# Attention within clusters, then a gated MLP: another searched order of one scheduled kernel, with other engines for splits, casts and code copies

## The chip, the cores and the metric

The kernel runs on one core of one Trainium2 chip. The metric is the device time of one execution in microseconds (us); less is better. TensorE multiplies matrices (PE in the profile, its weight loads PEld), VectorE is DVE, ScalarE is ACT, GpSimd is POOL, and SyncE (SP) issues most of the transfers.

## The reference

There are 4 batches of 8 heads, 768 positions and 64 channels per head, and 16 cluster centres per head. Each query and each key is assigned to the centre with the largest cosine; a query sees only the keys of its own cluster. The attention's result, 3072 rows of 512, goes through an MLP without biases.

```python
q_assign = np.argmax(np.einsum('bhsd,hcd->bhsc', q_n, c_n), axis=-1)
k_assign = np.argmax(np.einsum('bhsd,hcd->bhsc', k_n, c_n), axis=-1)
mask = q_assign[:, :, :, None] == k_assign[:, :, None, :]
scores = np.where(mask, scale * np.matmul(q, k.transpose(0, 1, 3, 2)), -1e9)
attn = softmax(scores)
x = (attn @ v).transpose(0, 2, 1, 3).reshape(B * S, H * D)      # 3072 x 512
h = x @ w_in                                                    # 512 -> 2048
out = (h * (1.0 / (1.0 + np.exp(-h)))) @ w_out                  # 2048 -> 512
```

## The kernel before

**Splits and turns.** Heads are worked on in pairs (p from 0 to 3 in each batch). `load_k`, `load_q` and `load_v` bring a pair's rows in; `load_v`'s second step casts V to 16 bits (`vt`, L431 on ScalarE, L433 on GpSimd or VectorE). `part` makes a pair ready: `hi` writes the scaled 16-bit value (L550 ScalarE, L552 VectorE, L554 GpSimd) and `lo` the remainder (L558, VectorE) into `hl`. Then `hl` is turned, channels on the partitions, into `ab`. For batch 0 TensorE does this by transposes, and another engine casts the result out of PSUM: in blocks of 8 (L584, cast by L593 or L595), or the older way by way of `lt` (L617, cast by L632 or L634), in which the cluster codes are turned by TensorE too (L617 once more, cast with a gain by L628 or L630). For batches 1 to 3, a DMA turns it (L573).

**Codes.** `logits` (L667, L671; L676 for later batches) multiplies by the centres; VectorE finds the largest (L718, or L694 and L714) and marks it (L743, or L726 on GpSimd, L753, L755). The marks are turned 32 by 32 on VectorE (`flip`, L771), and four copies per part (`put`, L786 ScalarE, L788 and L790 GpSimd, L792 and L794 VectorE) place them on partitions 64 to 79 of `ab`. So one matmul over 80 rows gives score and mask together.

**Attention.** For each head `scores` (L861) fills a PSUM bank with 512 scores, ScalarE takes the exponential (L868) into `P`, `pv` (L889) multiplies by V with a column of twos for the sum, VectorE divides (L902, L907), and the pair is turned into `xt` by a DMA (L926) or by TensorE (L937, cast by L942 or L944). Batch 0 is done in two rounds over the queries, blocks 0 and 1 first (24 exponentials), then 2 to 5 (48), so that the MLP can begin early.

**MLP.** `up` (L967) makes 16 blocks of 128 hidden channels, `tanh` (L973, ScalarE) and `gate` (L978, VectorE) the activation into `gq`, `down` (L1002) the result, which `leave` takes out of PSUM (L1015 ScalarE, L1017 VectorE) and SyncE stores (L1020). There are nine units of rows: three of 256 in batch 0, then two of 384 in each batch.

**What sets the order.** The kernel adds about 2,200 steps to a planner (`Plan`), each with an engine, an estimated duration, the steps it follows, the buffers it uses, and a key. `Plan.order` plays them through: the step that can start first goes next, and of equal ones that with the lower key. The instructions are then issued in that order, so each engine's queue is fixed at build time. Keys come from due times: `AT` (start of each round of attention), `ML` (start and end of each MLP unit) and `LEADS` (how far ahead of its use a part is made). `REST`, `RLOAD` and `SOON` say at which head of the attention a later part or load is let go. Where the planner sees TensorE idle before `UNREAD`, it puts in matmuls on zeros that nobody reads (L369); `MORE` lengthens such a fill. `FLIP` is time that it adds to a transposing DMA.

**Weights.** `w_in` comes in 4 pieces and `w_out` in 8, issued by GpSimd (L1036, L1040). Each waits for an event by reading one column of a tile into `pace` (L1034): `PW` gives for each piece the number of its event, 0 to 4 the `hi` steps of batch 0's keys, from 5 on every second exponential in the order in which the steps were added.

**Engine choices.** `VC` for the casts of batch 0's V by pair; `TK` for the casts of the turned blocks (entries 0 and 1 for the heads of pair 0, 2 to 4 for pairs 1 to 3); `TQ` for the codes, a word of four letters for four copies (P GpSimd, D VectorE, A ScalarE), or an engine's name for codes that TensorE turns; `TF` an extra engine for the first turn of a head done the older way; `TR` and `TS` the same as `TK` and `TQ` for the later queries of batch 0; `HI` and `HR` for `hi`; `PUTB` for later batches' codes; `XT` for the cast after L937; `EVAC` for `leave`, by unit.

```python
blocks = turn != "DMA" and turn[1] not in ("ACT", "DVE")
first_turns = [(c, his + los, turn[0]) for c in chunks]
if len(turn) > 2 and turn[2]:
    cut = runs[1][4]
    first_turns = [(chunks[0][:cut], [his[0], los[0]], turn[0]), (chunks[0][cut:], [his[1], los[1]], turn[2])]
```

Of the kernel before, what the change touches and what calls it, by code (L numbers as in the profile page):

```python
# [34 lines left out]
class Plan:  # L35
# [18 lines left out]
    def step(self, eng, w, fn, after=(), use=(), key=0.0, load=None, hold=0.0, pace=None, flip=False, lag=None, slack=0.0, port=None):  # L54
        s = Step()
        s.eng, s.w, s.fn, s.key, s.load, s.hold, s.flip = eng, w, fn, key, load, hold, flip
        s.lag = self.LAG.get(eng, 0) if lag is None else lag
        s.slack = slack
        s.port = eng == "POOL" if port is None else port
        s.use = list(use)  # L60
        s.n = len(self.steps)
        flat = []

        def gather(a):
            if isinstance(a, (list, tuple)):
                for x in a:
                    gather(x)
            elif a is not None:
                flat.append(a)

        gather(list(after))
        gather(pace)
        s.after = list({id(x): x for x in flat}.values())
        s.start = s.end = None
        for b in s.use:
            b.left += 1
        self.steps.append(s)
        return s
# [130 lines left out]
def kernel(  # L209
# [80 lines left out]
    def buf(name):  # L290
        return Buf(pools[name])
# [15 lines left out]

    SMALL = 30
    ISSUE = 470
    PW = [9, 6, 17, 12, 20, 21, 12, 6, 13, 25, 37, 25]  # L310
    UNREAD = 60000.0
    COLD = 8500.0
    MORE = 250.0
    LATE = 1500
    FLIP = 1200
    DONE = 0
    WSL = 1000
    AT = [-428.5, 146.6, 377.7, 476.2, 674.4, 872.8]
    ML = [144.4, 478.9, 304.3, 486.1, 673.0, 923.5, 414.3, 31.2, 1085.3, 1156.6]
    PUTB = ["POOL", "DVE", "POOL", "POOL"]  # L320
    VC = ["ACT", "POOL", "POOL", "DVE"]
    VB = "POOL"
    TK = ["DVE", "ACT", "ACT", "DVE", "ACT"]
    TQ = ["PPPD", "PPPA", "DVE", "PPPA", "PPPD"]
    TF = ["ACT", ""]
    TR = ["ACT", "DVE", "DVE", "DVE"]
    TS = ["PDPD", "PPPD", "PPPA", "PDPD"]
    RT = ["PE", "PE", "PE", "PE"]
    HI = ["POOL", "ACT", "POOL", "POOL"]
    HR = ["DVE", "POOL", "DVE", "POOL"]  # L330
    LEADS = [1401.7, 519.0, 568.3]
    REST = [1, 1, 10, 7]
    RLOAD = [0, 0, 0, 0]
    SOON = [6, 6, 5, 4]
    XT = ["DVE", "DVE", "DVE", "ACT"]
    XL = ["DMA", "DMA", "DMA"]
    EVAC = ["ACT", "DVE", "DVE", "DVE", "DVE", "DVE", "DVE", "DVE", "DVE", "ACT"]
    SPARE = 0
    FINE = 2

# [31 lines left out]

    plan.filler = (pools["M"], lambda t: 180.0 if t < COLD else 112.0, unread, UNREAD, MORE)

# [22 lines left out]
    def load_q(b, p, key, j0=0, j1=NJ, eng="SP", hs=(0, 1), pace=None):  # L397
        if (b, p) not in nqs:
            nqs[b, p] = buf("nq")
        x = nqs[b, p]  # L400

        def f():
            e = nc.sync if eng == "SP" else nc.scalar
            h0, h1 = 2 * p + hs[0], 2 * p + hs[-1] + 1
            e.dma_start(T["nq"][x.i][:, hs[0] : hs[-1] + 1, j0 * D : j1 * D], rows(q, b, h0, h1, j0, j1))

        s = step(eng, ISSUE, f, use=[x], key=key, load=105 * (j1 - j0) * len(hs), pace=pace, slack=LATE if b else 550 if eng == "ACT" else 0)
        for h in hs:
            for j in range(j0, j1):
                ld_q[b, p, h, j] = s  # L410
        return s
# [3 lines left out]
    def load_v(b, p, key, pace=None):  # L415
        eng = VC[p] if b == 0 else VB
        x = buf("nv")

        def f():
            nc.sync.dma_start(T["nv"][x.i], rows(v, b, 2 * p, 2 * p + 2, 0, NJ))  # L420

        s = step("SP", ISSUE, f, use=[x], key=key, load=1250, pace=pace, slack=LATE if b else 0)
        for h in range(2):
            y = buf("vt")
            vts[b, 2 * p + h] = y

            def g(h=h, y=y):
                dst = T["vt"][y.i][:, 0 : NJ * VW].rearrange("p (j c) -> p j c", c=VW)[:, :, 0:D]
                src = T["nv"][x.i][:, h, :].rearrange("p (j d) -> p j d", d=D)
                if eng == "ACT":  # L430
                    nc.scalar.copy(dst, src)  # L431
                else:
                    (nc.gpsimd if eng == "POOL" else nc.vector).tensor_copy(dst, src)  # L433

            w = {"POOL": pool_w(384), "ACT": act_w(384), "DVE": dve_w(384, 0.55)}[eng]

            cast_v[b, 2 * p + h] = step(eng, w, g, port=eng == "DVE", after=[s, s_ones], use=[x, y], key=key + 20)
# [57 lines left out]
    def part(b, p, segs, a0, due, lead=20.0, hi_eng="POOL", turn="DMA", twin=False, sub="POOL", code_eng=None, pace=None, wait=None):  # L495
# [73 lines left out]
        if turn == "DMA":  # L569
# [4 lines left out]

            turned = [step("SP", 120 * n, turn_dma, after=[his, los], use=[hl, A], key=key + 2 * span, load=195 * n, flip=True, slack=FLIP)]
        elif blocks:
# [245 lines left out]
    def attention(b, h, j0, j1, key, per, turn):  # L822
# [100 lines left out]
        if turn == "DMA":  # L923
# [6 lines left out]

            x = step("SP", 1240, turn_x, after=done, use=[xn, X], key=key + per - 3, load=195 * nq, flip=True, slack=FLIP)
        else:
# [96 lines left out]
    def weight(kind, n, event):  # L1029

        x, use, name, col = event

        def f():
            nc.gpsimd.tensor_copy(pace, T[name][use.i][:, col : col + 1])  # L1034
            if kind == "in":
                nc.gpsimd.dma_start(  # L1036
                    win_s[:, :, ts(n, 512)], moe_w_in.rearrange("(r p) f -> p r f", p=128)[:, :, ts(n, 512)]
                )
            else:
                nc.gpsimd.dma_start(  # L1040
                    wout_s[:, 2 * n : 2 * n + 2, :],
                    moe_w_out[256 * n : 256 * n + 256, :].rearrange("(c p) d -> p c d", p=128),
                )

        return step("POOL", 1210, f, after=[x], use=[use], key=-1, load=2390 if kind == "in" else 1190, slack=WSL)


    want = {(n, h): AT[n] + (AT[n + 1] - AT[n]) * h / H for n in range(NU + B - 1) for h in range(H)}

# [14 lines left out]
    for h in range(2):  # L1064
        part(
            0, 0, [("k", h, 0, NJ), ("q", h, 0, NA)], (NJ + NA) * h, want[0, h], lead=LEADS[0], hi_eng=HI[0],
            turn=(TK[h], TQ[h], TF[h]), wait=s_split if h else None, **engines,
        )
    for p in range(1, NP):
        part(  # L1070
            0, p, [("k", 0, 0, NJ), ("k", 1, 0, NJ), ("q", 0, 0, NA), ("q", 1, 0, NA)], 0, want[0, 2 * p], lead=LEADS[0],
            hi_eng=HI[p], turn=(TK[1 + p], TQ[1 + p]), wait=s_cent, **engines,
        )
# [3 lines left out]
    def at(place, f):  # L1077
        todo.setdefault(place, []).append(f)

    for p in range(NP):  # L1080
        at(RLOAD[p], lambda s, p=p: load_q(0, p, want[1, 2 * p] - 30, NA, NJ, pace=s))
        at(
            REST[p],
            lambda s, p=p: part(
                0, p, [("q", 0, NA, NJ), ("q", 1, NA, NJ)], 2 * (NJ + NA), want[1, 2 * p], lead=LEADS[1], pace=s,
                hi_eng=HR[p], **(engines | dict(turn=(TR[p], TS[p])) if RT[p] == "PE" else dict(code_eng=PUTB)),
            ),
        )
    for b in range(1, B):
        for p in range(NP):  # L1090
# [3 lines left out]
            for f, early in ((load_k, 32), (load_q, 31), (load_v, 30)):  # L1094
                at(place - (SOON[0] if soon else SOON[1]), lambda s, b=b, p=p, f=f, due=due - early: f(b, p, due, pace=s))
            for i in range(2):
                at(
                    place + i - (SOON[2] if soon else SOON[3]),
                    lambda s, b=b, p=p, i=i: part(
                        b, p, [("k", i, 0, NJ), ("q", i, 0, NJ)], 12 * i, want[b + NU - 1, 2 * p + i], lead=LEADS[2], pace=s, code_eng=PUTB  # L1100
                    ),
                )
    for place in range(H * (B + NU - 1)):
        n, h = divmod(place, H)
        per = (AT[n + 1] - AT[n]) / H
        if n < NU:
            j0, j1 = ROUNDS[n]
            attention(0, h, j0, j1, want[n, h], per, XT[p] if (p := h // 2) == NP - 1 or n + 1 < NU else "DMA")
        else:
# [4 lines left out]
    for n in range(4):  # L1114
        w_in_done.append(weight("in", n, events[PW[n]]))
    for n in range(8):
        w_out_done.append(weight("out", n, events[PW[4 + n]]))
    units = [(0, *r) for r in UNITS] + [(b, 3 * c, 3 * c + 3) for b in range(1, B) for c in range(2)]
    for n, (b, j0, j1) in enumerate(units):
        mlp(b, j0, j1, ML[n], ML[n + 1], lambda t, n=n: EVAC[n], n == len(units) - 1)  # L1120

# [31 lines left out]
```

## Time and profile before

| | us |
|---|---|
| median of 3 runs | 304.93 (304.78 to 305.57) |
| the profiled execution's own time | 306.86 |
| its span, first to last instruction | 304.9 |
| TensorE busy in the span | 295.9 |
| VectorE, ScalarE, GpSimd busy | 216.5, 216.4, 124.5 |
| granted TensorE clock | 1.00 throughout |

The profile is of one execution. "Busy" is the time in which an engine has at least one instruction under way; matmuls overlap, so a row's mean duration is longer than the distance from one start to the next. A row of the timeline gives start, length, engine, line, operation, output<-inputs, shapes, the number of instructions merged, and in brackets the idle time before it with what ended it. A row of the groups gives busy time and mean length, then the idle time before the group.

### The profile page before, as it was taken

How to read it: one execution, taken by the hardware profiler on the slowest of the kernel's cores; microseconds unless marked ns; L12 is line 12 of the kernel's file. 1: busy time of each engine (PE TensorE's matmuls, PEld its weight loads, DVE VectorE, ACT ScalarE, POOL GpSimd, SP SyncE). 2: the span in 40 equal slices, each digit the busy share in tenths (PEclk: the TensorE clock that was granted, in tenths of full speed). 3: DMA queues.
4: the chain of work that ended last, by engine and by line, in shares of the span. 5: the costliest groups of instructions: out<-in, count | busy, mean ns of one | idle time of the engine just before them, and what ended most of it. 6: DMA issues, size and time to landing. Idle time of an engine off the chain costs nothing.

```text
span 304.9 us, 8202 instructions
## 1 busy us (share of the span) xinstructions
PE 295.9 (97%) x3172; PEld 191.9 (63%) x3172; DVE 216.5 (71%) x523; ACT 216.4 (71%) x450; POOL 124.5 (41%) x248
## 2 busy tenths in 40 slices
PE   8999999989989999999999999999999999999996
PEld 6887766549667675566666666546765655544643
DVE  5998686768999899489869999935663357233842
ACT  2779999976999994599987999506999736200720
POOL 4799745571855866543485762250020000000000
DMA  6889997999298999549699697012210130003102
GB/s 217 269 206 232 191 150 141 276 205 271 60 245 217 180 229 243 146 109 180 189 168 267 165 174 106 3 69 60 54 28 19 46 88 9 0 34 120 54 33 73
DMA packets 71095, 42.12 MB, mean 138 GB/s; under 512 B 50448, under 2 KB 68112, under 8 KB 71056
## 3 DMA queue, kind: packets, MB, share of 16 engines
q1 hardware_dynamic: 66352, 37.23, 52.0%
q0 software_dynamic: 4288, 4.20, 9.2%
q8 instruction: 25, 0.41, 0.5%
q10 hardware_dynamic: 416, 0.16, 0.2%
q14 instruction: 14, 0.11, 0.1%
HBM read 27.30 MB, written 6.29 MB: 110 GB/s over the span
## 4 chain that ended last, share of the span: by engine, by line
PE 70%; DVE 13%; POOL 6%; DMA 5%; issue 3%; ACT 1%; POOLq 0%; DVEq 0%
PE bank L1002 24%; PE bank L967 23%; PE bank L861 12%; PE bank L889 7%; DVE hl L558 4%; DMA wout_s<-in_moe_w_out_dram 3%; DMA win_s<-in_moe_w_in_dram 3%; PE bank L369 2%; POOL ab L788 2%; POOL ab L790 2%; PE bank L676 2%; POOL hl L554 1%; DVE L L694 1%; DVE ohT L771 1%; DVE gq L978 1%
## 5 line engine op out<-in xcount | busy, mean ns | idle before, releaser
L868 ACT ACTIVATE P<-bank 128x512 f16<-128x512 f32 x288 | 157.3, 664 | 16.5 <-PE bank L861 16.0
L973 ACT ACTIVATE tn<-bank 128x384 f32<-128x384 f32 (+1 forms) x144 | 69.1, 491 | 49.3 <-PE bank L967 47.8
L1002 PE MATMUL bank<-wout_s,gq 128*128 128x512 f16 (+2 forms) x400 | 95.5, 370 | 2.1 <-DMA wout_s<-in_moe_w_out_dram 1.5
L967 PE MATMUL bank<-xt,win_s 128*128 128x384 f16 (+1 forms) x576 | 96.1, 308 | 0.6 <-DMA win_s<-in_moe_w_in_dram 0.6
L978 DVE SCALAR_TENSOR_TENSOR gq<-tn,bank 128x384 f16<-128x384 f32 (+1 forms) x144 | 71.1, 505 | 30.9 <-ACT tn L973 27.4
L861 PE MATMUL bank<-ab 80*128 80x256 f16 (+1 forms) x384 | 88.9, 325 | 1.9 <-DVE xn L907 0.9
L967 PEld LDWEIGHTS <-win_s 128*128 128x128 f16 x576 | 54.9, 97 | 29.9 <-DMA win_s<-in_moe_w_in_dram 1.1
L1002 PEld LDWEIGHTS <-gq 128*128 128x128 f16 x400 | 37.3, 98 | 38.3 <-issue 2.0
L788 POOL COPY ab<-ohT 16x384 f16<-16x384 f16 x72 | 40.4, 561 | 32.9 <-DVE ohT L771 18.7
L861 PEld LDWEIGHTS <-ab 80*128 80x128 f16 x384 | 34.7, 97 | 24.1 <-issue 1.6
L889 PEld LDWEIGHTS <-P 128*128 128x128 f16 x1152 | 43.7, 97 | 8.4
L889 PE MATMUL bank<-vt,P 128*128 128x65 f16 x1152 | 47.2, 193 | 0.0
L726 POOL TENSOR_TENSOR Df<-L,mx 128x192 f32<-128x192 f32 x24 | 13.4, 562 | 54.4 <-DVE mx L714 53.3
L1017 DVE COPY ot<-bank 128x512 f32<-128x512 f32 (+2 forms) x23 | 15.3, 665 | 24.9 <-PE bank L1002 23.5
L558 DVE SCALAR_TENSOR_TENSOR hl<-nq,hl 128x384 f16<-128x384 f32 (+3 forms) x33 | 22.8, 694 | 2.2 <-POOL hl L554 2.1
L907 DVE TENSOR_TENSOR xn<-bank,rz 128x384 f16<-128x384 f32 (+2 forms) x40 | 18.9, 474 | 1.0
L558 DVE SCALAR_TENSOR_TENSOR hl<-nk,hl 128x384 f16<-128x384 f32 (+1 forms) x29 | 19.2, 665 | 0.1
L771 DVE STREAM_TRANSPOSE ohT<-oh 128x384 f16<-128x384 f16 (+2 forms) x32 | 17.6, 553 | 0.3
L554 POOL TENSOR_SCALAR hl<-nk 128x384 f16<-128x384 f32 (+1 forms) x28 | 15.3, 547 | 5.2 <-DMA nk<-in_k_dram 4.3
L694 DVE TENSOR_REDUCE L<-bank 128x192 f32<-128x384 f32 x24 | 13.2, 550 | 5.5 <-PE bank L676 5.5
L433 POOL CAST vt<-nv 128x384 f16<-128x384 f32 x28 | 16.3, 607 | 0.6
L902 DVE RECIPROCAL rz<-bank 128x6 f32<-128x6 f32 (+2 forms) x40 | 7.1, 178 | 11.7 <-PE bank L889 11.5
(68 smaller groups left out, 183.7 us busy)
## 6 DMA issues: line engine op xcount, KB each, us to landing
nv<-in_v_dram SPq DMA_DIRECT2D x16, 384.0 KB, 5.7
out_dram<-ot SPq DMA_DIRECT2D x23, 256.0 KB, 2.1
nk<-in_k_dram SPq DMA_DIRECT2D x15, 384.0 KB, 4.2
nq<-in_q_dram SPq DMA_DIRECT2D x12, 384.0 KB, 4.7
win_s<-in_moe_w_in_dram POOLq DMA_DIRECT2D x4, 512.0 KB, 7.5
wout_s<-in_moe_w_out_dram POOLq DMA_DIRECT2D x8, 256.0 KB, 7.6
nq<-in_q_dram SPq DMA_DIRECT2D x4, 256.0 KB, 4.4
nk<-in_k_dram SPq DMA_DIRECT2D x2, 192.0 KB, 2.5
```

What stands on the lines that cost most here:

```text
L554: nc.gpsimd.tensor_scalar(out=dh, in0=src, scalar1=qs, scalar2=1.0, op0=ALU.mult, op1=ALU.mult)
L558: nc.vector.scalar_tensor_tensor(out=dl, in0=src, scalar=qs, in1=dh, op0=ALU.mult, op1=ALU.subtract)
L771: nc.vector.transpose(T["ohT"][ohT.i][:, 0:n, :].rearrange("p n c -> p (n c)"), T["oh"][oh.i][:, 0:n, :].rearrange("p n c -> p (n c)"),)
L788: nc.gpsimd.tensor_copy(dst, src)
L861: nc.tensor.matmul(banks[sb.i][:, at : at + 128 * (c1 - c0)], ab[0:80, kt[j], :], ab[0:80, qt + c0 : qt + c1, :].rearrange("p n c -> p (n ...
L868: nc.scalar.activation(out=T["P"][P.i][:, 0:at], in_=banks[sb.i][:, 0:at], func=AF.Exp, bias=0.0, scale=ESC if b else -ESC)
L889: nc.tensor.matmul(banks[O.i][:, (D + 1) * t : (D + 1) * t + nn], w, vt[:, VW * j : VW * j + nn], start=(j == 0), stop=(j == NJ - 1), skip ...
L907: nc.vector.tensor_tensor(out=T["xn"][xn.i][:, 0:nq, (h % 2) * D : (h % 2) * D + D], in0=banks[O.i][:, 0 : (D + 1) * nq].rearrange("p (t c ...
L967: nc.tensor.matmul(banks[bank.i][:, 0:n], win_s[:, r, ts(fb, 128)], T["xt"][xtb[b].i][:, r, 128 * j0 : 128 * j1], start=(r == 0), stop=(r ...
L973: nc.scalar.activation(out=T["tn"][tn.i][:, 0:n], in_=banks[bank.i][:, 0:n], func=AF.Tanh, bias=0.0, scale=1.0)
L978: nc.vector.scalar_tensor_tensor(out=T["gq"][g.i][:, fb % 4, 0:n], in0=T["tn"][tn.i][:, 0:n], scalar=1.0, in1=banks[bank.i][:, 0:n], op0=A ...
L1002: nc.tensor.matmul(banks[bank.i][:, 0 : c1 - c0], T["gq"][gqs[fc // 4].i][:, fc % 4, ts(t, 128)], wout_s[:, fc, c0:c1], start=(fc == 0), s ...
```

## The change

Only the planner's numbers and the engine choices change; no function does. In the queues this comes to the following. Head 1 (the second of pair 0) has its codes turned by TensorE instead of pair 2 (`TQ`): L617 issues 16 transposes for 32, L584 88 for 80, and the second head's keys and queries are cast by ScalarE in two steps of 768 and 256 columns. Of the casts of turned blocks ScalarE does 6 (4 before) and VectorE 5 (6 before, and 2 more by L630); ScalarE casts V for pairs 0 and 1 of batch 0, GpSimd for pairs 2 and 3. Pair 1's `hi` moves from ScalarE to GpSimd, pair 2's from GpSimd to ScalarE. Copies of batch 0's codes: GpSimd 28 (22 before), VectorE 2 (7), ScalarE 2 (3). Of 25 output copies ScalarE does 11 (2 before), VectorE 14 (23). Fillers: 59 (53). Weights: pieces 0 and 2 of `w_in` and piece 4 of `w_out` wait for the same split of pair 2's keys, piece 1 of `w_in` for an exponential of head 6. The order of all queues changes with the due times; in round two of batch 0 pair 1 goes first, and in later batches the pairs' buffers differ.

```diff
-    PW = [9, 6, 17, 12, 20, 21, 12, 6, 13, 25, 37, 25]
-    UNREAD = 60000.0
+    PW = [3, 15, 3, 11, 6, 28, 24, 12, 3, 16, 31, 36]
+    UNREAD = 80000.0
     COLD = 8500.0
-    MORE = 250.0
+    MORE = 120.0
     LATE = 1500
-    FLIP = 1200
+    FLIP = 1800
...
-    AT = [-428.5, 146.6, 377.7, 476.2, 674.4, 872.8]
-    ML = [144.4, 478.9, 304.3, 486.1, 673.0, 923.5, 414.3, 31.2, 1085.3, 1156.6]
-    PUTB = ["POOL", "DVE", "POOL", "POOL"]
-    VC = ["ACT", "POOL", "POOL", "DVE"]
+    AT = [-179.6, -158.1, 86.3, 263.5, 510.0, 780.3]
+    ML = [-346.1, 272.3, -79.5, 273.8, 532.7, 887.5, 180.9, 687.8, 766.8, 1323.5]
+    PUTB = ["DVE", "POOL", "POOL", "POOL"]
+    VC = ["ACT", "ACT", "POOL", "POOL"]
     VB = "POOL"
-    TK = ["DVE", "ACT", "ACT", "DVE", "ACT"]
-    TQ = ["PPPD", "PPPA", "DVE", "PPPA", "PPPD"]
-    TF = ["ACT", ""]
-    TR = ["ACT", "DVE", "DVE", "DVE"]
-    TS = ["PDPD", "PPPD", "PPPA", "PDPD"]
+    TK = ["ACT", "ACT", "ACT", "ACT", "DVE"]
+    TQ = ["PPPP", "ACT", "PPPA", "PPPA", "PPPP"]
+    TF = ["", "ACT"]
+    TR = ["DVE", "ACT", "DVE", "DVE"]
+    TS = ["PPPD", "PPPP", "PPPP", "PPPD"]
     RT = ["PE", "PE", "PE", "PE"]
-    HI = ["POOL", "ACT", "POOL", "POOL"]
-    HR = ["DVE", "POOL", "DVE", "POOL"]
-    LEADS = [1401.7, 519.0, 568.3]
-    REST = [1, 1, 10, 7]
-    RLOAD = [0, 0, 0, 0]
-    SOON = [6, 6, 5, 4]
-    XT = ["DVE", "DVE", "DVE", "ACT"]
+    HI = ["POOL", "POOL", "ACT", "POOL"]
+    HR = ["POOL", "DVE", "DVE", "DVE"]
+    LEADS = [931.4, 795.2, 77.1]
+    REST = [7, 2, 4, 5]
+    RLOAD = [4, 0, 0, 3]
+    SOON = [9, 5, 8, 4]
+    XT = ["ACT", "DVE", "DVE", "ACT"]
     XL = ["DMA", "DMA", "DMA"]
-    EVAC = ["ACT", "DVE", "DVE", "DVE", "DVE", "DVE", "DVE", "DVE", "DVE", "ACT"]
+    EVAC = ["DVE", "ACT", "DVE", "DVE", "ACT", "DVE", "ACT", "ACT", "DVE", "ACT"]
```

## The prediction

> **What bounds the kernel now.** I read the page first, then the busy time by stage, then TensorE's own timeline wherever a stage leaves it idle.
>
> ```profile
> PE 295.9 (97%) x3172; PEld 191.9 (63%) x3172; DVE 216.5 (71%) x523; ACT 216.4 (71%) x450; POOL 124.5 (41%) x248
> PE   8999999989989999999999999999999999999996
> DVE  5998686768999899489869999935663357233842
> ACT  2779999976999994599987999506999736200720
> ```
>
> The busy time by stage (us of each engine, then granted clock, DMA share, GB/s):
>
> ```profile
> 0.00:30.00 30.00, 27.94 (x438) 23.07 (x439) 25.59 (x79) 21.05 (x35) 23.02 (x57) 1.00 0.84 232
> 30.00:60.00 30.00, 29.28 (x394) 20.36 (x393) 21.93 (x62) 29.38 (x68) 17.29 (x35) 1.00 1.09 185
> 60.00:121.00 61.00, 57.80 (x729) 40.95 (x728) 53.71 (x135) 51.19 (x113) 37.90 (x72) 1.00 0.95 206
> 121.00:302.00 181.00, 180.88 (x1616) 107.55 (x1613) 115.00 (x250) 114.83 (x236) 46.30 (x87) 1.00 0.40 93
> 302.00:305.00 3.00, 0.00 (x0) 0.00 (x0) 0.28 (x1) 0.00 (x0) 0.00 (x0) 1.00 0.27 87
> ```
>
> The first column after the stage's length is TensorE. From 121 us to the end of the last matmul it idles 0.12 us in 181: what ScalarE, VectorE or GpSimd do there costs nothing unless one of them falls far behind, and they are near 115 of 181. Of the 9.0 us that TensorE idles in the whole span, 2.9 are the tail after the last matmul and 6.0 lie before 121 us. Beside these, 10.1 us of its busy time are filler matmuls, on zeros, that nobody reads (the group below). So the end is set by one sum: useful matmuls (295.9 - 10.1 = 285.8), plus fillers, plus idle time, 304.9. An order can move only the last two, 19.1 us. The idle stretches before 121 us, with what ended them:
>
> ```profile
> 29.76 0.59 PE L861 MATMUL bank<-ab 80*128 80x512 f16 x2
> 41.85 0.61 PE L967 MATMUL bank<-xt,win_s 128*128 128x256 f16 x4 [0.62 <-DMA win_s<-in_moe_w_in_dram]
> 66.72 1.02 PE L1002 MATMUL bank<-wout_s,gq 128*128 128x512 f16 x4 [1.48 <-DMA wout_s<-in_moe_w_out_dram]
> 88.05 0.81 PE L861 MATMUL bank<-ab 80*128 80x512 f16 x4 [0.92 <-DVE xn L907]
> 117.97 1.04 PE L1002 MATMUL bank<-wout_s,gq 128*128 128x512 f16 x4 [0.64 <-DVE gq L978]
> ```
>
> The first row is round two of batch 0: the last filler stands just before it, so up to there the start-up chain sets the pace. Then come two waits for weights and two for VectorE.
>
> **The change part by part.** *Fewer transposes.* Pair 2's codes no longer go through TensorE (32 transposes by L617), the second head's do (16); L584 rises from 80 to 88. Eight transposes fewer:
>
> ```profile
> L584 PE MATMUL bank<-ident,hl 128*128 128x128 f16 x80 | 5.8, 219 | 0.1
> L369 PE MATMUL bank<-zeros 128*128 128x256 f16 x53 | 10.1, 347 | 1.0 <-DVE zeros L347 1.0
> ```
>
> 5.8 / 80 is 0.07 us, so -0.6. The fillers go from 53 to 59. They stand in waits before round two, so six more (0.19 us each by the row, 1.1 in all) cost 0; with that cover gone, 1.1.
>
> *The start-up.* What was on VectorE (cast of head 0's turned block, pair 2's code turn, most of the code copies) goes to ScalarE and GpSimd, pair 1's split goes from ScalarE to GpSimd and pair 2's the other way.
>
> ```profile
> 6.78 0.63 PE L584 MATMUL bank<-ident,hl 128*128 128x128 f16 x8
> 6.55 0.84 ACT L550 ACTIVATE hl<-nk 128x768 f16<-128x768 f32 x1 [4.55 <-DMA nk<-in_k_dram]
> 7.67 0.42 ACT L550 ACTIVATE hl<-nq 128x256 f16<-128x256 f32 x1 [0.27 <-DMA nq<-in_q_dram]
> 10.21 0.93 ACT L431 CAST vt<-nv 128x384 f16<-128x384 f32 x2 [0.81 <-DMA nv<-in_v_dram]
> 11.28 1.93 ACT L632 COPY lt<-bank 128x1024 f16<-128x1024 f16 x2
> 13.67 1.57 ACT L868 ACTIVATE P<-bank 128x512 f16<-128x512 f32 x3 [0.46 <-PE bank L861]
> 17.19 1.93 ACT L593 COPY ab<-bank 128x1024 f16<-128x1024 f16 x2
> 12.95 1.29 DVE L595 COPY ab<-bank 128x1024 f16<-128x1024 f16 x2
> 19.06 0.69 DVE L771 STREAM_TRANSPOSE ohT<-oh 128x512 f16<-128x512 f16 x1
> 16.35 0.98 POOL L1036 DMA_DIRECT2D win_s<-in_moe_w_in_dram  x1
> 17.42 1.32 POOL L790 TENSOR_SCALAR ab<-ohT 16x256 f16<-16x256 f16 x3
> 18.80 1.22 POOL L433 CAST vt<-nv 128x384 f16<-128x384 f32 x2
> 21.15 2.30 POOL L790 TENSOR_SCALAR ab<-ohT 16x512 f16<-16x512 f16 x3
> ```
>
> ScalarE can start when the first eight transposes end, at 7.4. Ahead of its first exponential now stand five casts of 1024 (4.8), two of 768 and 256 (1.2, an estimate between the cast of 1024 and nothing), the split of pair 2 (1.26), three casts of V (1.4) and the second head's gain cast (1.0 by the cast of 1024): 9.7 us, so 17.1 instead of 13.67. That isn't yet a loss. By the same rows GpSimd waits with its first weight issue for ScalarE's split of pair 2 (ends about 10.1), then issues (0.98), places head 0's codes (1.32 for three) and splits pair 3, to 13.7; pair 1's logits follow 0.8 of matmuls after pair 2's turn, near 14.6, its peaks and marks take 0.8, VectorE's cast 0.65 and the turn by VectorE 0.69, so that its codes are ready at 17.1. From there GpSimd's queue is the chain: pair 1's three copies (2.3) to 19.4, pair 2's (2.3) to 21.7, two casts of V (1.2) and a weight issue (0.9) to 23.8, pair 3's four copies (3.1) to 26.9, two casts (1.2) to 28.1, then pair 1's four short copies for round two (1.75): 29.9 to 30.2. Round two started at 29.76 before; the changed order has 0.4 us more useful matmuls ahead of it. Term: 0, between -1.3 (GpSimd's two casts and one issue hidden) and +1.5 (ScalarE's lag carried on).
>
> *Weights.* GpSimd paces them by other events: pieces 0 and 2 of w_in very early, piece 1 only after all the copies above and pair 2's (10 in all), near 32.7. Rows of the chain that ended last, and of the landing times of w_in:
>
> ```profile
> 34.18 7.63 DMA win_s<-in_moe_w_in_dram
> 57.83 8.86 DMA wout_s<-in_moe_w_out_dram
> DMA to landing us min/median/max: 5.7/7.5/9.6
> ```
>
> Piece 1 lands at 38.4 by the shortest and 40.2 by the median. TensorE reaches block 4 of the up product, the first that needs it, 6.9 us of matmuls after round two starts: 37.3. I take 1.1 us, since less is on the queues by then, for the 0.62 of before: +0.5, from -0.6 to +2.3. The last piece of w_out hangs on the third exponential of head 6 in round two, whose scores stand after 42 us of useful matmuls; with the 13.5 us that TensorE is behind by then, and 0.7 for ScalarE, that is 56.2, 1.6 earlier than the issue of before at 57.83, while its user moves little: of 1.48 I leave 0.4, -1.1, from -1.5 to +0.5.
>
> *VectorE relieved.* Nine evacuations of the output go to ScalarE:
>
> ```profile
> L1017 DVE COPY ot<-bank 128x512 f32<-128x512 f32 x21 | 14.4, 688 | 22.7 <-PE bank L1002 21.3 <-DMA out_dram<-ot 1.3
> L1015 ACT COPY ot<-bank 128x512 f32<-128x512 f32 x2 | 1.2, 586 | 1.5 <-PE bank L1002 1.5
> 54.69 0.46 PE L676 MATMUL bank<-stk,ab 128*128 128x32 f16 x12
> 60.86 0.38 PE L861 MATMUL bank<-ab 80*128 80x512 f16 x1
> ```
>
> VectorE loses 9 x 0.69 = 6.2 us there, ScalarE gains 9 x 0.59 = 5.3, nearly all after 121 us, where both have room: 0. Of the two waits for VectorE before 121 us (0.92 and 0.64) I take away half, -0.8, from -1.6 to 0.
>
> *New tight places.* The last two rows are the first logits of batch 1 and the scores that use them: 5.9 us from the end of the one to the other, and TensorE had just enough else to do. In the changed order 5.0 us of matmuls stand between the second head's logits of that pair and its scores: +0.6, from 0 to +1.5. And in the up products of round two four banks come back after 1.5 to 1.75 us of matmuls, while ScalarE is behind: +0.3, from 0 to 1.5.
>
> Sum: -0.6 + 0 + 0.5 - 1.1 - 0.8 + 0.6 + 0.3 = -1.1, a span of 303.8. The profiled execution took 306.86 for its span of 304.9, and the median of the runs shown is 304.93; I carry the difference over to the median: 303.8.
>
> **The rivals.** *ScalarE becomes the bound (slower).* It is busy 29.38 of 30 us from 30 to 60. By the rows above 3.1 us more ScalarE work stands ahead of batch 1's first exponential: two casts of 1024 (1.9), two of V (0.9) and the gain cast (1.0), less 0.7 for the shorter turn of head 1. It pays that from what it idled before 13.67. If it idles by more than 1 us between 7.4 and 17, every us after that reaches TensorE; I price it at 2.5 above the time of before, 307.4. For it: the pair 1 casts wait for turns that wait for VectorE. Against: in that stage TensorE idles only 0.72 us of 30, and 0.62 of it for a weight, so it is the bound there and ScalarE the second. Chance 0.19.
>
> *The early weights take the loads' place (slower).* The q loads of 256 KB took 4.4 us in the median, and 7.6 when a piece of w_in was under way:
>
> ```profile
> nq<-in_q_dram SPq DMA_DIRECT2D x4, 256.0 KB, 4.4
> nq<-in_q_dram SPq DMA_DIRECT2D x1, 256.0 KB, 7.6
> ```
>
> In the changed order three pieces fly between 10 and 22 us, over the q rows of round two and pair 2's and 3's V. Those have some 2 us to spare before their casts; a slip of over 2 us stops GpSimd's queue, which carries the start, and sends piece 1 of w_in later too (its 2.3). Price 1.0 + 2.3 on the time of before, less the 1.1 that I found: 307.1. Chance 0.17. The Trainium skill ("DMA: Bandwidth & Descriptors", section "SWDGE vs HWDGE vs iDMA") says that GpSimd's queue and the others' feed different internal queues of each DMA engine, which serves them in turn. The two rows agree: near half speed. By that rule the slip is 3.2 us for each load that a piece overlaps, and the rival would hold.
>
> *The start gains (faster).* Pair 2's scores can come at 21.7 for 23.5 before; if GpSimd's queue runs 1.3 us ahead of my count, round two does too: 302.5. Chance 0.16. *Gains and losses cancel,* and the order does nothing: 304.9, chance 0.12.
>
> **How the numbers follow.** My forecast, 303.8, has 0.36, with its own range 302.9 to 304.9; three quarters of it lie over 0.3% below 304.93 (about what a measurement of this kernel can tell from no change). Faster: 0.27 + 0.16 = 0.43. Same: 0.09 + 0.06 = 0.15. Slower: 0.19 + 0.17 + half of the cancelling case, 0.06, is 0.42. The signs are nearly even, so the range takes in both: 301.0, where the start gains and the weights come in time, to 309.0, where ScalarE's lag and the late piece add up in part.
>
> **What would show it.** Right: the last filler before 31 us; ScalarE's first exponential near 17; a wait for w_in near 37 and one of under 1 us for w_out near 63; no idle TensorE after 121. Wrong: fillers or gaps after 32 us, score matmuls that wait for exponentials' banks between 30 and 60, or waits of TensorE for codes after 64 us that add to over 3 us.

## The result and the profile after

The changed kernel took 302.49 us (302.20 to 302.97, 4 runs), the kernel before 305.03 (304.78 to 305.57, 4 runs): ratio 0.9916, 95% interval 0.9897 to 0.9935. Forecast were 303.8 us, 1.1 below the kernel before, and a range of 301.0 to 309.0; the measured gain is 2.5. Profiled anew beside before, it had 0.9911 (0.9880 to 0.9943). The profiled execution took 302.20 us, its span 300.4.

The same lines of the page as shown of before, then the busy time by stage (the last row ends with the last matmul), then TensorE's groups of transposes and fillers:

```profile
PE 293.8 (98%) x3170; PEld 192.0 (64%) x3170; DVE 206.5 (69%) x504; ACT 224.7 (75%) x464; POOL 126.3 (42%) x253
PE   8899999999999999999999999999999999999996
DVE  6879876759998894799878794677662343453342
ACT  2999999987899994899889874798898543563120
```
```profile
0.00:30.00 30.00, 27.46 (x454) 23.53 (x455) 24.27 (x72) 24.60 (x42) 23.78 (x58) 1.00 1.00 271
30.00:60.00 30.00, 29.63 (x387) 20.59 (x386) 22.35 (x64) 29.29 (x67) 20.83 (x44) 1.00 0.98 160
60.00:121.00 61.00, 60.60 (x737) 42.66 (x734) 49.56 (x127) 51.58 (x115) 35.20 (x65) 1.00 0.87 199
121.00:297.40 176.40, 176.03 (x1601) 105.19 (x1599) 110.05 (x243) 119.28 (x242) 46.46 (x88) 1.00 0.37 95
```
```profile
L369 PE MATMUL bank<-zeros 128*128 128x256 f16 x59 | 10.1, 319 | 1.0 <-DVE zeros L347 1.0
L584 PE MATMUL bank<-ident,hl 128*128 128x128 f16 x88 | 6.4, 220 | 0.0
```

From 60 to 121 us TensorE is busy 60.60 of 61 (57.80 before), and VectorE has 49.56 us of work (53.71 before). All the idle times of TensorE after 10 us whose end its timeline puts down to somebody:

```profile
14.56 0.39 PE L861 MATMUL bank<-ab 80*128 80x256 f16 x2 [0.99 <-POOL ab L790]
24.96 0.18 PE L667 MATMUL bank<-stk,ab 128*128 128x16 f16 x1 [0.31 <-ACT ab L593]
30.24 0.59 PE L861 MATMUL bank<-ab 80*128 80x512 f16 x2 [0.21 <-POOL ab L790]
34.65 0.29 PE L937 MATMUL bank<-ident,xn 128*128 128x128 f16 x2 [0.16 <-DVE xn L907]
82.81 0.38 PE L861 MATMUL bank<-ab 80*128 80x256 f16 x2 [0.40 <-DVE xn L907]
170.91 0.59 PE L861 MATMUL bank<-ab 80*128 80x512 f16 x3 [0.28 <-DVE ot L1017]
```

No wait for a weight is left. Of those for VectorE between 60 and 121 us (0.92 and 0.64 before) one of 0.40 is left; one of 0.28 at 170.91 is new. From the starts of all matmuls I work out TensorE's *delay*: how far a matmul starts behind the sum of what the useful matmuls ahead of it take from start to start (217 ns for 512 columns, 163 for 384, 109 for 256, 55 for 128, 30 for 65, 25 below, as undisturbed neighbours show). Fillers and idle time both raise it. "Again" is the kernel before, profiled once more (below).

| delay (us) at | before | before, again | after |
|---|---|---|---|
| 32 us | 12.75 | 12.34 | 12.86 |
| 60 us | 14.26 | 13.83 | 13.22 |
| 121 us | 18.58 | 17.08 | 13.95 |
| last matmul | 18.63 | 17.14 | 14.61 |
| useful matmuls | 283.15 | 283.15 | 282.71 |
| span | 304.9 | 303.5 | 300.4 |

### The profile page after: what moved, and what is told of

Read it like the earlier page. It is cut to its first block, busy times and chain, and to the rows that moved or that the text cites. A ratio compares the mean times of both kernels' runs of the same rounds, so it can differ in the third digit from the quotient of the medians.

```text
span 300.4 us, 8210 instructions
## 1 busy us (share of the span) xinstructions
PE 293.8 (98%) x3170; PEld 192.0 (64%) x3170; DVE 206.5 (69%) x504; ACT 224.7 (75%) x464; POOL 126.3 (42%) x253
## 4 chain that ended last, share of the span: by engine, by line
PE 87%; ACT 4%; DMA 3%; DVE 2%; POOL 2%; issue 1%; SPq 0%; POOLq 0%; ACTq 0%; DVEq 0%
PE bank L1002 28%; PE bank L967 26%; PE bank L861 19%; PE bank L889 10%; DMA nk<-in_k_dram 3%; ACT P L868 2%; PE bank L676 2%; POOL ab L790 1%; ACT tn L973 1%; PE bank L584 1%; PE bank L369 0%; DVE xn L907 0%; PE bank L667 0%; POOL hl L554 0%; PE bank L671 0%
## 5 line engine op out<-in xcount | busy, mean ns | idle before, releaser
L1002 PE MATMUL bank<-wout_s,gq 128*128 128x512 f16 (+2 forms) x400 | 97.3, 371 | 0.0
L967 PE MATMUL bank<-xt,win_s 128*128 128x384 f16 (+1 forms) x576 | 95.2, 308 | 0.1
L973 ACT ACTIVATE tn<-bank 128x384 f32<-128x384 f32 (+1 forms) x144 | 66.6, 487 | 36.8 <-PE bank L967 32.8
L978 DVE SCALAR_TENSOR_TENSOR gq<-tn,bank 128x384 f16<-128x384 f32 (+1 forms) x144 | 69.4, 501 | 33.9 <-ACT tn L973 30.4
L967 PEld LDWEIGHTS <-win_s 128*128 128x128 f16 x576 | 54.9, 97 | 27.6 <-issue 0.4
L788 POOL COPY ab<-ohT 16x384 f16<-16x384 f16 x72 | 38.2, 530 | 33.5 <-DVE ohT L771 16.4
L558 DVE SCALAR_TENSOR_TENSOR hl<-nk,hl 128x384 f16<-128x384 f32 (+1 forms) x29 | 22.0, 759 | 4.7 <-POOL hl L554 4.5
L1017 DVE COPY ot<-bank 128x512 f32<-128x512 f32 (+2 forms) x14 | 9.1, 648 | 16.1 <-PE bank L1002 16.1
L554 POOL TENSOR_SCALAR hl<-nk 128x384 f16<-128x384 f32 (+1 forms) x28 | 15.7, 560 | 2.7 <-DMA nk<-in_k_dram 1.9
L790 POOL TENSOR_SCALAR ab<-ohT 16x256 f16<-16x256 f16 (+1 forms) x28 | 15.7, 561 | 2.5 <-DVE ohT L771 0.6
```

Of the source, the lines that this page charges most:

```text
L558: nc.vector.scalar_tensor_tensor(out=dl, in0=src, scalar=qs, in1=dh, op0=ALU.mult, op1=ALU.subtract)
L788: nc.gpsimd.tensor_copy(dst, src)
L790: nc.gpsimd.tensor_scalar(out=dst, in0=src, scalar1=gain_, scalar2=1.0, op0=ALU.mult, op1=ALU.mult)
L967: nc.tensor.matmul(banks[bank.i][:, 0:n], win_s[:, r, ts(fb, 128)], T["xt"][xtb[b].i][:, r, 128 * j0 : 128 * j1], start=(r == 0), stop=(r ...
L973: nc.scalar.activation(out=T["tn"][tn.i][:, 0:n], in_=banks[bank.i][:, 0:n], func=AF.Tanh, bias=0.0, scale=1.0)
L978: nc.vector.scalar_tensor_tensor(out=T["gq"][g.i][:, fb % 4, 0:n], in0=T["tn"][tn.i][:, 0:n], scalar=1.0, in1=banks[bank.i][:, 0:n], op0=A ...
```

## The experiments

Unless said otherwise the order of all queues is frozen as the planner gave it, and only the edit differs. `order` is `plan.order()`, which is then issued step by step. Each ratio is to the kernel before on the same chip, whose median was 305.4 to 305.9.

**Weights.** The changed kernel, unchanged:

> The changed kernel, unchanged, profiled once more: 302.5, ratio 0.9905, no wait for a weight, and no more than 1 us between the shortest and the longest run, since what made before spread (landings that TensorE waits for) is not on its path; rival: the spread comes from the start, and is as wide as that of before, 1.5 us and more.

302.77, 0.9911 (0.9880 to 0.9943), from 302.32 to 303.41 in 7 runs (1.1 us, just over the 1 expected), no wait for a weight. The kernel before, unchanged:

> The kernel before, unchanged, profiled once more. The first profile of it took 306.86 us, 1.9 more than its median of 305.0. Theory W (weights): the waits for w_in (0.62 at 41.85) and w_out (1.48 at 66.72) come in every run: 305.0, and the new profile shows both within 0.3 us. Rival C (chance): the wait for w_out was an accident of that one execution: a profile near 305.0 shows less than 0.4 us of it.

305.74 us, 0.9992 (0.9970 to 1.0014); the profiled execution 305.5.

```profile
41.42 0.61 PE L967 MATMUL bank<-xt,win_s 128*128 128x256 f16 x4 [0.77 <-DMA win_s<-in_moe_w_in_dram]
65.23 1.46 PE L1002 MATMUL bank<-wout_s,gq 128*128 128x512 f16 x6 [0.41 <-DMA wout_s<-in_moe_w_out_dram]
86.56 1.02 PE L861 MATMUL bank<-ab 80*128 80x512 f16 x5 [0.92 <-DVE xn L907]
116.48 1.90 PE L1002 MATMUL bank<-wout_s,gq 128*128 128x512 f16 x8 [0.64 <-DVE gq L978]
```

The two waits for VectorE came back to the hundredth, that for w_in with 0.77 for 0.62; that for w_out fell from 1.48 to 0.41. Chance (C) is the nearer for w_out, though it had named less than 0.4, and W for w_in. Neither holds strictly: in the seven further profiles below in which both are unmoved, w_out's wait was 0 (in two) to 0.89, w_in's 0 (in one) to 1.08.

```diff
+    order = plan.order()
+    late, lead = w_out_done[6], w_out_done[7]
+    late.fn = early      # piece 6, paced by the exponential of piece 7
+    order.remove(late)
+    order.insert(order.index(lead) + 1, late)
```

> The kernel before with its order kept, but piece 6 of w_out issued right behind piece 7 (at 44.5 us instead of 57.83), after the same exponential as piece 7. By the landing times of its neighbours (4.6 to 5.0 us) it lands near 50, and its user comes after 66. No wait for w_out in either theory. W: the 1.48 us come out of the time, less what the next step takes back: 303.6 to 304.0, ratio 0.996. C: 304.8, ratio 0.999.

304.97, 0.9979 (0.9966 to 0.9991): 0.6 us. The wait for w_out is gone. Nearer to C (0.999); W's 0.996 is outside the interval.

```diff
+    TURN = [0, 1, 2, 3, 4, 5, 6, 7, 12, 13, 14, 15, 8, 9, 10, 11]
             def up(fb=fb, bank=bank):
+                if b == 0 and j0 == 0:
+                    fb = TURN[fb]
```

(The gate likewise.)

> The kernel before with its order kept, but in the first MLP unit blocks 12 to 15 of the up product are done before blocks 8 to 11. Piece 3 of w_in landed at 35.17, piece 2 at 41.81, and the fifth to eighth blocks after the swap come 2 us of matmuls and more behind 41.85. So the wait of 0.62 goes. W: 0.6 goes from this place, but the wait for w_out, whose landing hangs on exponentials that ScalarE gives at its own pace, takes most of it back: 304.4 to 305.0. C: nothing takes it back: 304.4.

304.55, 0.9969 (0.9953 to 0.9985): 0.9 us, no wait for w_in, and 0.25 for w_out. The gain stayed, as C has it.

The same edit in the changed kernel puts 4 to 7 ahead of 8 to 11:

> The changed kernel with its order kept, but in the first MLP unit the up blocks go in the order of their numbers, 4 to 7 ahead of 8 to 11 (the change did 8 to 11 first). TensorE reaches the fifth block at 37.5, and piece 1 of w_in landed at 38.90. W: a wait of 1.4 us for w_in appears near 37.5, and all of it reaches the end, since TensorE idles nowhere behind it for a weight: 303.9, ratio to before 0.996. Rival (ScalarE and VectorE are the second bound of this stage and use the time to catch up): half of it comes back, 303.2.

304.16, 0.9956 (0.9939 to 0.9973), 1.4 above the changed kernel by the ratios (0.9956 - 0.9911 = 0.0045 of 306). Its timeline (L970 is the changed kernel's L967, three lines further down):

```profile
39.07 1.05 PE L970 MATMUL bank<-xt,win_s 128*128 128x256 f16 x8 [1.16 <-DMA win_s<-in_moe_w_in_dram]
```

That is the wait the prediction feared. The change escapes it because its order does blocks 8 to 11, whose piece landed at 21.68, before 4 to 7. W holds: from 60 us to the last matmul the delay grows as in the changed kernel (1.55 us, 1.54 there), so none of the wait is made up. The medians alone, with these intervals, don't exclude the rival's half.

**VectorE's queue.**

```diff
+    for n, anchor, behind in [(569, 568, 1), (1580, 1579, 1)]:
+        order.remove(by_n[n])
+        order.insert(order.index(by_n[anchor]) + behind, by_n[n])
```

> The kernel before with its order kept, but two instructions of VectorE go earlier in its queue: one normalisation (L907, at 85.94 in the newest profile) right behind its reciprocal, ahead of a turn, two remainders and a code copy; one gate (L978, at 116.00) right behind its tanh, ahead of a code copy, an output copy and a reduction. VectorE's work is the same. Theory Q (TensorE waits for a place in VectorE's queue): the waits of 1.08 and 0.80 us that TensorE shows there go, -1.9, 303.6, ratio 0.994. Rival R (VectorE has too much work in this stage; relief by other engines is what counts): what is pushed back is late next, -0.5 at most, ratio 0.998.

304.71, 0.9983 (0.9953 to 1.0012). The wait at 116.5 is gone; the other keeps its size and changes its releaser:

```profile
87.36 0.59 PE L861 MATMUL bank<-ab 80*128 80x256 f16 x3 [0.92 <-DVE gq L978]
```

Q holds at 116 us, R at 87: there the gate that was pushed back became what TensorE waits for. The time is R's (0.998); Q's 0.994 is outside the interval.

```diff
-            def leave(bank=bank, ot=ot, eng=eng, w=c1 - c0):
+            def leave(bank=bank, ot=ot, eng=LEAVE[units.index((b, j0, j1))], w=c1 - c0):
```

> The kernel before with its order kept, but the output copies go by the changed kernel's list (11 on ScalarE, 14 on VectorE; before 2 and 23). R: half of the two waits for VectorE between 60 and 121 us goes, -0.8 and more, ratio 0.997. Q: only two of the nine moved copies lie before 121 us, and those of the first unit go the other way; both waits stay within 0.2 us: ratio 1.000.

306.32, 1.0037 (1.0010 to 1.0065): no relief, rather 1 us worse, which neither theory had. The first unit's two copies go to VectorE, which has four output copies for three and 55.71 of 61 us to do there (54.74 before, again); by the delay its trace waits for VectorE 0.4 us longer in this stage and 0.35 longer at 176 us. The reverse, in the changed kernel:

> The changed kernel with its order kept, but the output copies go by the list of before (2 on ScalarE, 23 on VectorE). Theory O (the nine copies have no part in the gain; VectorE is eased between 60 and 121 us because the new order does one head's preparation less in that stage): 302.5, within 0.4, ratio to before 0.990. Theory E (ScalarE's output copies are what eases VectorE): the waits for VectorE come back, 303.3 or more, ratio 0.993.

303.21, 0.9923 (0.9897 to 0.9949), 0.44 above the changed kernel beside it (302.77). Between the two theories: the copies have a part of about 0.4, with the difference's own uncertainty, in the 2 us that the waits for VectorE lost (worked out below).

> The kernel before with three local edits together: piece 6 of w_out early, blocks 12 to 15 ahead of 8 to 11 in the first unit, and the two moves in VectorE's queue. If the terms add (w_in 0.93, w_out 0.57, VectorE 1.9 by the newest profile of before): -3.4, 302.1, ratio 0.989, as fast as the changed kernel or a little faster, with none of its engine choices. If they don't add (what TensorE gains early it waits for later, behind ScalarE): -2.0 or less, ratio 0.9935.

303.82, 0.9938 (0.9917 to 0.9959). The terms don't add: 2.0 of 3.4. Three local edits give some two thirds of the change's gain (0.0062 of 0.0089 by the ratios) without any of its engine choices. Waits for VectorE at 78 to 86 us are left.

**Which engine's work?** VectorE's code copies of later batches on GpSimd:

```diff
-                    elif puts[g] == "POOL" and not blocks:
+                    elif not blocks:
                         nc.gpsimd.tensor_copy(dst, src)
```

> The kernel before with its order kept, but the code copies of batches 1 to 3 that VectorE did (L792, 10 of 0.45 us between 60 and 121 us, one straight ahead of each of the two late instructions) are done by GpSimd at the same places. That takes 4.5 us of VectorE's work out of the stage, about as much as the changed kernel has less there (54.74 against 49.56). If work in the stage is what counts: the waits of 1.08 and 0.80 go, -1.5 to -1.9, ratio 0.994. If only the place in the queue counts: each shrinks by the 0.45 in front of it, -0.9, ratio 0.997. Against both: GpSimd's copies come later and scores wait for codes (0.33 at 101.87 before), up to +0.5.

307.50, 1.0068 (1.0044 to 1.0093): slower by 1.8 us, against both theories. Scores stand idle 1.03 at 103 us for codes that GpSimd now places late (0.16 before, again): the third possibility, and more than the 0.5 it was given. What VectorE waited for from 60 to 121 us, two rows of that kernel, then the same two of before, profiled again:

```profile
DVE hl L558 <- POOL hl L554: 5.6, 7, 2.4
DVE oh L755 <- POOL Df L726: 3.0, 4, 1.8
```
```profile
DVE hl L558 <- POOL hl L554: 1.5, 1, 1.5
DVE oh L755 <- POOL Df L726: 1.1, 2, 0.7
```

VectorE has 6 us less work in the stage (48.60 for 54.74) and waits 6.0 longer for GpSimd, in order behind its splits and differences, which come later. The Trainium skill ("Perfetto Trace Analysis", section "Optimizing Scalar/DVE Operations") says that moving operations between these two might not help, since they share a read port; here it did harm. What the rows show is the wait in the queue; a part of the port was not measured apart.

> The three local edits of before (weight piece early, blocks swapped, two places in VectorE's queue) and the code copies of VectorE on GpSimd. Without the last edit it took 303.8 (ratio 0.994), with waits for gates of VectorE left between 70 and 90 us (0.43, 0.30, 0.53) and one of 0.33 at 48.5. If VectorE's work in the stage is what is left: these 1.3 us at 70 to 90 go, 302.5, ratio 0.990, the changed kernel's time. If not: 303.8, ratio 0.994.

306.82, 1.0050 (1.0030 to 1.0070): 3.0 worse than without it by the medians, 3.4 by the ratios, against both expectations again.

```diff
-                if eng == "ACT":
+                if eng == "ACT" or b:
                     nc.scalar.copy(dst, src)
```

> The kernel before with its order kept, but V of batches 1 to 3 is cast by ScalarE and not by GpSimd (L433, 12 casts between 60 and 121 us, 0.57 us each in GpSimd's queue). It is the mirror of before_puts: GpSimd loses 6.8 us of 38.9 in that stage, VectorE does the same. Theory G (VectorE waits in its queue for GpSimd's differences and splits, and TensorE for what stands behind them): VectorE's waits for GpSimd (1.5 and 1.1) go, TensorE's waits of 1.08, 0.33 and 0.80 shrink to half, -1.1, ratio 0.9965. Theory V (VectorE's own work): no change, ratio 1.000. Rival A: ScalarE, at 50.8 of 61 us, has 6 more, and exponentials come late: slower by 1 us and more, ratio 1.003.

309.10, 1.0106 (1.0076 to 1.0136). Rival A: ScalarE has 56.69 of 61 us there, and by the delay scores wait for banks that exponentials free at 51, 52, 66, 148 and 184 us (0.25 to 0.55 each, 1.8 in sum; the time lost is 3.7).

Two casts behind one difference on GpSimd, `[(542, 531, 1), (543, 542, 1)]` in the form above:

> The kernel before with its order kept, but at 81.2 us two casts of V on GpSimd go behind the difference (L726) for which VectorE waited 0.72 at 82.64. No work is moved to another engine. G: VectorE's queue up to the late normalisation runs 0.7 earlier, and TensorE's wait of 1.08 at 86.56 falls to 0.4 or less, ratio 0.998. V: the wait stays at 1.0 to 1.1, ratio 1.000.

305.71, 1.0003 (0.9979 to 1.0026). VectorE's wait fell to 0.37, and by the delay TensorE's at 87 us from 1.08 to 0.70, but waits for gates of 0.42 and 0.30 came at 80.0 and 81.7 in its place: 1.4 in sum (with 0.70), where these gates and the normalisation had 1.25 before. Neither G nor V had that, and the interval holds the ratios of both.

So the work was left out instead of moved, in two kernels that use older values in its place:

```diff
                     elif not blocks:
-                        nc.vector.tensor_copy(dst, src)
+                        pass
```

> The kernel before with its order kept, with VectorE's code copies of batches 1 to 3 left out (L792; a quarter of the queries and keys of each head keeps older codes, and nothing else takes the work). Theory V (VectorE's own work between 60 and 121 us, 54.74 of 61, sets TensorE's waits for it there): the waits of 1.25 between 78 and 88 us and of 0.80 at 116.5 go, -1.9, ratio 0.994. Theory G (GpSimd's queue sets them): each late instruction gains only the 0.45 that stood in front of it, -0.9, ratio 0.997.

303.78, 0.9956 (0.9931 to 0.9981): 1.3 us.

> The kernel before with its order kept, with 22 of 24 casts of V of batches 1 to 3 left out (L433 on GpSimd; the products use older values of V, and nothing else takes the work). G: VectorE's waits for GpSimd go and TensorE's with them, 1.25 between 78 and 88 and half of the 0.80 at 116.5, and 0.33 at 101.9: -1.9, ratio 0.994. V: only the 0.72 that VectorE idled at 82.64 is won, -0.5, ratio 0.998.

305.24, 1.0002 (0.9978 to 1.0026): nothing. From 60 to 121 us, first the kernel without VectorE's code copies, then the one without GpSimd's casts, then before, again:

```profile
60.00:121.00 61.00, 60.12 (x742) 42.11 (x741) 50.87 (x127) 50.36 (x112) 39.11 (x73) 1.00 1.02 213
60.00:121.00 61.00, 59.78 (x738) 41.77 (x737) 54.81 (x138) 51.24 (x113) 33.72 (x62) 1.00 1.01 215
60.00:121.00 61.00, 58.87 (x734) 41.43 (x733) 54.74 (x137) 50.77 (x113) 38.92 (x73) 1.00 0.98 212
```

With VectorE at 50.87 (the changed kernel has 49.56) the delay grows by 1.6 in this stage, 0.4 of it for w_out; with GpSimd at 33.72 and VectorE at 54.81 by 2.5, 0.3 of it for w_out; before by 3.25, 0.57 of it for w_out. So without VectorE's copies TensorE loses 1.5 us less to anything but weights, without GpSimd's casts 0.5 less. The times alone say less: the first interval holds the ratios of both theories, and the profile of the first kernel also lacks the wait for w_in, which its edit doesn't touch; the second rules out G's 0.994. VectorE's own work sets most of these waits (V); GpSimd's share is small.

**A faster version.** The changed kernel with two moves in VectorE's queue, `[(614, 564, 1), (1790, 1246, 0)]`:

> The changed kernel with its order kept, but a reciprocal and a normalisation go ahead of a remainder (at 81.21) in VectorE's queue, and an output copy ahead of a remainder (at 169.43). Q: the two waits of TensorE behind them (0.56 at 82.81, 0.44 at 170.91) go: 1.0 off its 302.5, 301.5, ratio to before 0.986 to 0.989. R: 302.3, ratio 0.991.

301.49, 0.9865 (0.9841 to 0.9889), and once more:

> The changed kernel with the two earlier places in VectorE's queue and nothing else, beside the others on one chip: 301.5, ratio 0.9865.

301.94, 0.9877 (0.9850 to 0.9905). Its ten runs lie from 301.42 to 302.38, the changed kernel's eleven from 302.20 to 303.41. Q holds where VectorE has room: both waits are gone, and TensorE is busy 61.00 of 61 us from 60 to 121 us. The largest loss that is left is the start:

```diff
-                    elif puts[g] == "ACT":
+                    elif puts[g] == "ACT" and not blocks:
+    order.remove(w_out_done[0])
+    order.insert(order.index(w_in_done[3]) + 1, w_out_done[0])
```

> The changed kernel with the two earlier places in VectorE's queue (301.5 with these alone), and two edits at the start: piece 0 of w_out is issued behind piece 3 of w_in (0.95 us less on GpSimd ahead of round two), and two code copies go from ScalarE to VectorE (1.24 less on ScalarE, 0.6 more on VectorE). If GpSimd and ScalarE set the start: round two starts 0.4 to 0.9 earlier than 30.4, 300.8, ratio 0.984. If VectorE's queue does: 301.5 or a little more, ratio 0.9865.

302.90, 0.9912 (0.9887 to 0.9937): 1.0 worse than beside it without the edits. From the first scores to round two it takes 16.2 us (30.88 - 14.67), without the edits 15.7, and TensorE now waits for VectorE's marks and remainders (0.36, 0.36, 0.64 between 18 and 27 us) and 0.6 at 39.57 for a code copy on GpSimd behind the moved issue. So half of the loss arises before round two, where VectorE has the two copies more, and half at that wait. VectorE's queue seems to limit the start as well; the two edits were not tried apart, and which of the three engines could spare anything there stays open.

## Why the prediction was right or wrong

The sign was right and the sum was not: -1.1 was forecast, -2.5 came. Read from the delays, the repetition of before against the changed kernel, the terms in the order of the forecast's sum came out as follows.

| term (us) | forecast | measured |
|---|---|---|
| fewer transposes | -0.6 | -0.4 |
| start | 0 | +0.5 |
| w_in | +0.5 | -0.9 |
| w_out | -1.1 | -0.6 |
| VectorE relieved | -0.8 | -1.95 |
| new tight places | +0.9 | 0 |
| after 121 us | 0 | +0.6 |

They add to -2.8; the two spans differ by 3.1. Three steps failed: w_in had the wrong sign, the relief of VectorE was less than half of what came and had the wrong cause, and the tight places cost nothing. That the sum missed by only 1.4 is in part luck, since the start and the stage after 121 us took back 1.1 that the forecast had at nothing.

- *Fewer transposes, -0.6:* the useful matmuls shrank by 0.44. About right. The 59 fillers cost nothing, the last at 26.7.
- *The start, 0:* the path was right. Round two came at 30.24 (forecast 29.9 to 30.2), by GpSimd's queue as worked out. In delay at 32 us that is 0.1 more than in the profile used, 0.5 more than in its repetition. ScalarE's first exponential came at 15.46, not 17.1: ScalarE began 0.8 sooner, and its instructions start closer together than their durations add up to (two casts of V of 0.51 each took 0.93 in the row of before). Nothing hung on that.

```profile
6.56 1.01 ACT L593 COPY ab<-bank 128x1024 f16<-128x1024 f16 x1 [4.55 <-PE bank L584]
15.46 0.61 ACT L868 ACTIVATE P<-bank 128x512 f16<-128x512 f32 x1
```

- *w_in, +0.5:* the step that failed first, and the furthest. Issue (33.46 for 32.7) and landing (38.90 for 38.4 to 40.2) were right, but "the first that needs it" was taken from the numbers of the blocks; the order issues 8 to 11 ahead of 4 to 7. With 4 to 7 first, the wait of 1.16 did come (after_blocks_in_order). As it was, the wait of before, 0.6 in the profile used and 0.9 in the delay of its repetition, went altogether: 1.1 to 1.4 us from the term.
- *w_out, -1.1:* right in place (55.85 for 56.2) and too large for a usual run. It landed in 4.7 us (the lines below), not 8.9, or 7.8 in the repetition of before; six loads of 384 KB were issued around it before, from 54.6 to 59.4 us, and come from 60.1 on after. That these made it slow was not tried alone. But most of the 1.48 to be won was that one execution's: 0.6 was what moving the piece was worth.

```profile
L1040 POOL DMA_DIRECT2D wout_s<-in_moe_w_out_dram x1: 762/762/762, 55.9 to 55.9; - x1
...
DMA to landing us min/median/max: 4.7/4.7/4.7
```

- *VectorE relieved, -0.8:* right in sign, mis-sized, and with the wrong cause. 1.95 us went (3.25 - 0.57 for w_out, against 0.73). The prediction took half of the two waits away for nine output copies that it had itself put after 121 us, nearly all of them; no row gave the half. From 60 to 121 us VectorE has one output copy more, not fewer. What it has less is about one head's preparation. Turns, code copies and output copies there, of the changed kernel and of before, again:

```profile
L771 DVE STREAM_TRANSPOSE ohT<-oh 128x384 f16<-128x384 f16 x9 | 5.1, 572 | 0.1
...
L792 DVE COPY ab<-ohT 16x384 f16<-16x384 f16 x9 | 3.0, 331 | 0.3
L1017 DVE COPY ot<-bank 128x512 f32<-128x512 f32 x4 | 2.7, 686 | 0.8 <-PE bank L1002 0.8
```
```profile
L771 DVE STREAM_TRANSPOSE ohT<-oh 128x384 f16<-128x384 f16 x10 | 5.7, 571 | 0.1
...
L792 DVE COPY ab<-ohT 16x384 f16<-16x384 f16 x11 | 4.3, 388 | 0.3
...
L1017 DVE COPY ot<-bank 128x512 f32<-128x512 f32 x3 | 2.1, 692 | 0.1
```

That VectorE's load is what counts is shown by leaving 3.9 us of it out, which took 1.5 us of delay away (before_no_puts). That the head's preparation is what the change took away is read from these rows; it was not tried alone. The copies' list as a whole has about 0.4 (after_evac_before).

- *New tight places, +0.6 and +0.3:* neither came. No score waited for the second head's logits at 64 us, and the delay moved by less than 0.1 from 36 to 60 us. I had bounded each by its distance in matmuls and taken a middle value for a distance that was "just enough"; no row showed a wait. (By the two rows that distance is 5.7 us, from 54.69 + 0.46 to 60.86, and not 5.9.)
- *After 121 us, 0:* 0.6 lost (waits of 0.25 at 140.66 and 0.44 at 170.91 by the delay). Missed. The faster version wins the second back, not the first.
- *The carried difference:* the profiled execution of before was 1.9 us above its own median, and the waits read from it were taken for those of every run. Between the two first profiles the span fell by 4.5, between the medians 2.5.
- *Rivals.* ScalarE is not the bound: 29.29 of 30 us from 30 to 60, but TensorE 29.63. The q loads took longer with the weights early, 6.0 for 4.4 as the row of issues shows, but up to round two no engine stood waiting for one of them. "The start gains" gave 302.5, the time that came, for a reason that did not happen: that is luck.

```profile
nq<-in_q_dram SPq DMA_DIRECT2D x4, 256.0 KB, 6.0
```

## What to carry to other kernels

Profile the kernel before twice, and keep as a term only the waits that come back; a wait for a transfer may not (1.48, then 0.41). Read the order in which blocks are used from the queue, not from their numbers. Where an engine is near full in a stage (here VectorE, 54.7 of 61 us), an instruction moved ahead in its queue, or work handed to the neighbour, can just move the wait; work that leaves the stage takes waits away, and leaving some out for one run helps to tell whose work it was.

## What was not expected of the hardware

VectorE's mark of 96 values (L753) takes 0.20 us or 0.56, by what GpSimd does at the time: from 60 us on, 13 of them with GpSimd idle took 0.20 in the median (before, again), the 6 with GpSimd busy for nine tenths of the time 0.56. One of each, of the changed kernel and of before, again:

```profile
83.11 0.20 DVE L753 TENSOR_SCALAR oh<-Df 128x96 f16<-128x96 f32 x1
```
```profile
83.06 0.56 DVE L753 TENSOR_SCALAR oh<-Df 128x96 f16<-128x96 f32 x1
```

And the kernels that wait for landings spread more from run to run: the kernel before ran from 304.7 to 307.3 us in 28 of 29 runs of one set (the other took 309.6). Of those with no such wait, before_all ran from 303.5 to 304.1 in 6, before_all_puts from 306.6 to 307.6 in 12, the changed kernel from 302.2 to 303.4 in 11. That the landings make the spread is likely, but not shown: these kernels differ in more than that.
